# Taking the fourth head group's visit early, moving three half results to another buffer, and redrawing the scheduling settings in a fused attention and MLP kernel

## The chip, the cores and the metric

One core of one Trainium2 chip runs the whole program. The metric is the device time of one execution in microseconds. The engines are named as in the profile: PE (matmuls), PEld (the weight loads of PE), ACT (ScalarE), DVE (VectorE), POOL and SP (which issues the transfers). The kernel before took 1079.97 us, the median of 6 runs.

## The reference

It is a transformer block over 2048 tokens of width 1024: 32 query heads of width 32 that share one key and one value head, then an MLP with a sigmoid gate, each behind a layer norm and inside a residual sum.

```python
q = (ln(x) @ wq) -> 32 heads of 32;  k = ln(x) @ wk;  v = ln(x) @ wv      # one k, one v
p = softmax(q @ k.T * 32**-0.5);     h = x + (p @ v) @ wo
out = h + (sigmoid(ln(h) @ w_gate) * (ln(h) @ w_up)) @ w_down             # inner width 3584
```

## The kernel before

The program is built by a greedy planner that runs before compilation. It keeps an estimated clock for each engine and appends one instruction at a time to each engine's fixed list. Work on a query tile of 128 tokens is cut into **visits** (G, kq): head group G (8 heads of one query tile, so four groups make a tile) with key pair kq (256 keys). A visit is 8 score matmuls of 32 rows each and two exponentials of 128x1024. The first visits run while queries and keys are still being computed:

```python
visits = [(0, 0), (1, 0), (2, 0), (0, 1), (1, 1), (2, 1), (0, 2), (1, 2), (0, 3), (1, 3),
          (2, 2), (3, 0), (2, 3), (3, 1), (3, 2), (3, 3)]
visits += [(G, kq) for G in range(NX) for kq in range(VPH, VPG)]          # NX = 4: second halves
visits += [(G, kq) for G in range(NX, NT * ND) for kq in range(VPG)]
```

The first four groups are taken in two halves. The first half's result (values and row sums, 128x512 float32) is parked until the second half is there. Three lie in h_sb, the residual buffer, and the fourth in tnh:

```python
OcX = h_sb[...].bitcast(F32)                                 # three slots of 512 float32
def ocx(G, a, b):
    return OcX[:, G, a:b] if G < NH else tnh[:, a:b]         # NH = 3
```

Many instructions copy PSUM out, on ACT or on DVE, whichever is expected to be free first. One rule says how much queued work is counted:

```python
def evac(fn_act, fn_dve, n, deps, prio, dve_rate=0.96):
    now = pl.free["pe"]
    ready = now + 300.0 if v < 2 else 1e9                    # v: visits emitted so far
    a = max(pl.free["act"], now) + sum(o.occ for o in pl.heap["act"] if o.ready <= ready) + n / 1.2
    d = max(pl.free["dve"], now) + sum(o.occ for o in pl.heap["dve"] if o.ready <= ready) + n / dve_rate
    if a + (1000.0 * KNOBS[v // WIN][3] if v else 0.0) < d:  # ... ACT, else DVE
```

KNOBS holds 65 tuples of eight small integers, one tuple for each eight visits. They set thresholds and break ties in the planner. When nothing is ready for PE, the planner puts in **fillers**, matmuls whose result nobody reads:

```python
if 0 < v < 16 and not spare and known([exps[2 * v - 1]], t):
    ... mm(S_ps[:, k, 0:P], ident[:, :], ident[:, :], True, True), [c_id, exps[2 * v - 1]] ...
if v and spare:
    ... mm(F_ps[:, spare[0], 0:256], ident[:, :], kT4[:, 0:256], True, True) ...
```

The softmax here doesn't subtract the row's maximum and nothing guards it: scores larger than these inputs give would overflow.

## Time and profile before

| | before |
|---|---|
| median of 6 runs | 1079.97 us (1079.74 to 1080.29) |
| span of the profiled run | 1078.0 us |
| ACT busy, 60 to 1016 us | 955.18 of 956 us |
| last exponential ends | 1015.9 us |
| PE alone after that | 62 us |

A span is the time from the first to the last instruction, some 2 us less than the device time.

### The profile page before, as it was taken

To read this page: it belongs to the slowest core of one execution; us is meant where nothing else is said; L and a number is where in the kernel's file an instruction comes from. 1 tells how busy PE (TensorE), PEld (TensorE's weight loads), DVE (VectorE), ACT (ScalarE), POOL (GpSimd) and SP (SyncE) were. 2 spreads that over 40 slices of the span, in tenths; PEclk is the share of its full clock that TensorE was granted. 3 is DMA by queue.
4 is the path that set the end of the run, shared out by engine and by line. 5 is a ranking of instruction groups with operands and counts; after the bars stand their busy time and mean duration, and the time that the engine had idled before them with its cause. 6 is when DMAs were issued, how large, how long until landed. Compare 5 with 4: busy or idle time off the path is not lost.

```text
span 1078.0 us, 31453 instructions
## 1 busy us (share of the span) xinstructions
PE 1043.5 (97%) x12925; PEld 489.3 (45%) x13094; DVE 903.2 (84%) x1736; ACT 1009.8 (94%) x1167; POOL 30.6 (3%) x58
## 2 busy tenths in 40 slices
PE   8999999999999999999999999999999999999999
PEld 7764434444444444444444444444444444444445
DVE  7899999898989879898888989898887988888721
ACT  6999999999999999999999999999999999999700
POOL 2100000000000000000000000000000000000000
PEclk9999999999999999999999999999999999999999
DMA  7997898929679695959879594955969489896994
GB/s 222 183 293 249 209 290 237 280 70 286 164 210 240 153 262 125 267 141 253 198 187 261 138 267 113 285 161 157 265 164 276 109 232 199 208 234 161 294 277 106
DMA packets 308623, 227.14 MB, mean 211 GB/s; under 512 B 119808, under 2 KB 299904, under 8 KB 308480
## 3 DMA queue, kind: packets, MB, share of 16 engines
q1 hardware_dynamic: 307296, 224.92, 81.8%
q8 instruction: 103, 1.69, 0.7%
q14 instruction: 40, 0.33, 0.1%
q10 hardware_dynamic: 1184, 0.20, 0.1%
HBM read 195.17 MB, written 7.86 MB: 188 GB/s over the span
## 4 chain that ended last, share of the span: by engine, by line
PE 73%; ACT 19%; issue 4%; DVE 2%; DMA 1%; SPq 0%; DVEq 0%
PE F_ps L415 57%; ACT Pr L707 18%; PE S_ps L415 16%; ACT tnh L1009 1%; DVE Ts L741 1%; DMA ring<-in_B_w_up_dram 1%; DVE Rc L806 0%; DMA ring<-in_A_x_dram 0%; DVE st L346 0%; DVE Oc L796 0%; DVE hact L291 0%; DVE st L348 0%; PE F_ps L444 0%; DVE Oc L291 0%; DVE Ts L748 0%
## 5 line engine op out<-in xcount | busy, mean ns | idle before, releaser
L707 ACT ACTIVATE Pr<-S_ps 128x1024 bf16<-128x1024 f32 x1024 | 968.9, 1156 | 3.3 <-PE S_ps L415 2.6
L741 DVE TENSOR_TENSOR Ts<-Ts,Pr 128x1024 bf16<-128x1024 bf16 x736 | 481.5, 677 | 33.7 <-ACT Pr L707 31.4
L415 PE MATMUL F_ps<-ring,hnT 128*128 128x512 bf16 (+1 forms) x1870 | 400.7, 380 | 13.1 <-issue 8.5
L415 PEld LDWEIGHTS F_ps<-ring,hnT 128*128 128x128 bf16 (+1 forms) x1957 | 147.6, 97 | 189.5 <-issue 48.3
L415 PE MATMUL S_ps<-QTb,kT 32*128 32x256 bf16 x4096 | 206.2, 273 | 1.2
L415 PE MATMUL F_ps<-zone,hact 128*128 128x512 bf16 (+2 forms) x1106 | 197.5, 377 | 9.5 <-issue 9.0
L415 PEld LDWEIGHTS S_ps<-QTb,kT 32*128 32x128 bf16 x4096 | 63.1, 92 | 206.3 <-ACT Pr L707 153.4
L415 PE MATMUL F_ps<-Pr,Vb 128*32 128x256 bf16 x4064 | 134.2, 274 | 0.3 <-issue 0.3
L415 PEld LDWEIGHTS F_ps<-zone,hact 128*128 128x128 bf16 (+1 forms) x1164 | 75.0, 97 | 83.5 <-issue 23.0
L415 PEld LDWEIGHTS F_ps<-Pr,Vb 128*32 128x32 bf16 x4064 | 96.8, 96 | 29.9 <-issue 17.0
L741 DVE TENSOR_TENSOR Ts<-Pr 128x1024 bf16<-128x1024 bf16 x128 | 86.6, 684 | 25.6 <-ACT Pr L707 25.1
L1013 DVE SCALAR_TENSOR_TENSOR hst<-tnh,F_ps 128x512 bf16<-128x512 f32 x107 | 73.3, 685 | 38.3 <-PE F_ps L415 36.4
L1009 ACT ACTIVATE tnh<-F_ps 128x512 f32<-128x512 f32 x105 | 77.5, 738 | 5.7 <-PE F_ps L415 5.7
L415 PE MATMUL F_ps<-zone 128*128 128x256 bf16 (+4 forms) x658 | 72.2, 272 | 2.3 <-issue 1.1
L415 PE MATMUL F_ps<-wo_sb,OT 128*128 128x512 bf16 (+1 forms) x283 | 58.4, 380 | 1.7 <-issue 1.6
L415 PEld LDWEIGHTS F_ps<-zone 128*128 128x128 bf16 (+1 forms) x667 | 43.1, 97 | 22.8 <-issue 7.4
L748 DVE TENSOR_TENSOR Ts<-Ts 128x1024 bf16<-128x1024 bf16 x64 | 43.9, 686 | 1.1
L358 POOL TENSOR_SCALAR zb<-mvb 128x1 bf16<-128x1 bf16 (+1 forms) x25 | 9.9, 397 | 993.6 <-DVE mvb L350 993.6
L1009 ACT ACTIVATE tnh<-S_ps 128x512 f32<-128x512 f32 x7 | 4.2, 597 | 35.3 <-PE S_ps L415 35.3
L291 DVE COPY Oc<-F_ps 128x256 f32<-128x256 f32 x60 | 25.3, 422 | 11.6 <-PE F_ps L415 10.7
L415 PEld LDWEIGHTS F_ps<-wo_sb,OT 128*128 128x128 bf16 (+1 forms) x294 | 21.0, 97 | 26.2 <-issue 6.8
L796 DVE TENSOR_TENSOR Oc<-F_ps,Oc 128x256 f32<-128x256 f32 x59 | 24.9, 423 | 7.5 <-PE F_ps L415 6.4
(84 smaller groups left out, 415.4 us busy)
## 6 DMA issues: line engine op xcount, KB each, us to landing
ring<-in_B_w_gate_dram SPq DMA_DIRECT2D x318, 256.0 KB, 4.8
ring<-in_B_w_up_dram SPq DMA_DIRECT2D x316, 256.0 KB, 4.6
zone<-in_B_w_down_dram SPq DMA_DIRECT2D x28, 256.0 KB, 3.7
h_sb<-in_A_x_dram SPq DMA_DIRECT2D x16, 256.0 KB, 4.5
out_dram<-h_sb SPq DMA_DIRECT2D x31, 128.0 KB, 3.0
ring<-in_A_x_dram SPq DMA_DIRECT2D x7, 512.0 KB, 5.3
QTb<-q_scratch SPq DMA_DIRECT2D x14, 256.0 KB, 5.4
Pr<-in_B_w_gate_dram SPq DMA_DIRECT2D x10, 256.0 KB, 4.1
```

Of the source, the lines that this page charges most:

```text
L291: lambda: DVE.tensor_copy(out=out_ap, in_=in_ap))
L358: f = pl.op("pool", lambda: POOL.tensor_scalar(out=zb[:, ph, sl].unsqueeze(2), in0=mvb[:, ph, sl, 1:2], scalar1=LN_EPS_BF16, scalar2=None, ...
L415: fn = lambda: PE.matmul(o, lhsT=l, rhs=r, start=start, stop=stop, **kw)
L707: exps[u] = pl.op("act", lambda slot=slot, pb=pb: ACT.activation(out=pslot(slot).rearrange("p (a b) -> p a b", a=2), in_=S_ps[:, pb:pb + 2 ...
L741: o = pl.op("dve", lambda T=T, a=a, b=b: DVE.tensor_tensor(out=T, in0=a, in1=b, op=ALU.add), deps, prio=4, **t_dve(1024, 1.92))
L748: merge_ev[G] = pl.op("dve", lambda T4=T4: DVE.tensor_tensor(out=T4[:, :, 0, :], in0=T4[:, :, 0, :], in1=T4[:, :, 1, :], op=ALU.add), [sum ...
L796: a = pl.op("dve", lambda: DVE.tensor_tensor(out=Oc[:, :], in0=O, in1=Ob, op=ALU.add), [last, oc_ev[G], o_ev.get(G - 1)], prio=0, **t_dve( ...
L1009: tanh_of[n] = pl.op("act", lambda: ACT.activation(out=tnh[:, :], in_=FB(b), func=ACTF.Tanh, scale=0.5), [last, tn_user.get(0)] + (tn_more ...
L1013: e = pl.op("dve", lambda: DVE.scalar_tensor_tensor(out=hst[:, n % NST, :], in0=tnh[:, :], scalar=1.0, in1=FB(b), op0=ALU.add, op1=ALU.mul ...
```

## The change

The intent: keep ACT fed in the head by a visit that needs only keys already there, copy more of the early PSUM results on DVE, keep h_sb free of half results, and fit the tuples to the new course. The tuples are cut; the rest is whole.

```diff
-    KNOBS = [(4, 7, 0, 2, 2, 0, 0, 0), (0, 4, 0, 4, 1, 0, 0, 0), ...   # 65 tuples
+    KNOBS = [(4, 7, 1, 1, 3, 0, 0, 0), (3, 4, 1, 4, 3, 2, 0, 0), ...   # 65 other tuples
+        OcH = [hact[:, P + k * D:P + (k + 1) * D].bitcast(F32) for k in range(3)]
+        assert P + 3 * D <= NFT * P
         def ocx(G, a, b):
-            return OcX[:, G, a:b] if G < NH else tnh[:, a:b]
+            if G == 3:
+                return tnh[:, a:b]
+            return OcX[:, G - 3, a:b] if G > 3 else OcH[G][:, a:b]
-            ready = now + 300.0 if v < 2 else 1e9
+            ready = now + 300.0 if v < 4 else 1e9
-                    queues["Q" if t else "Q0"].append(mk_Q2(g, t))
+                    queues["Q0" if t == 0 or g < 2 * (NX - ND) else "Q"].append(mk_Q2(g, t))
-        visits = [(0, 0), (1, 0), (2, 0), (0, 1), (1, 1), (2, 1), (0, 2), (1, 2), (0, 3), (1, 3),
-                  (2, 2), (3, 0), (2, 3), (3, 1), (3, 2), (3, 3)]
+        visits = [(0, 0), (1, 0), (2, 0), (3, 0), (0, 1), (1, 1), (2, 1), (0, 2), (0, 3), (1, 2),
+                  (1, 3), (2, 2), (3, 1), (2, 3), (3, 2), (3, 3)]
+        visits += [(G, kq) for G in range(4, NX) for kq in range(VPH)]
         def xr_ready(t, deps):
-            if t < NH:
-                load_xr(t, deps)
-            else:
+            if t < 3:
+                oc_used.extend(deps)
+            elif t == 3:
                 tn_user[0] = deps[0]
                 tn_more.extend(deps[1:])
+            else:
+                load_xr(t - 3, deps)
+            if t == 2:
+                for k in [0] + list(range(NX - 3, NH)):
+                    load_xr(k, [])
+        oc_used = []
-                    [e] + ([d_last[t - 2]] if t > 1 else q_store[-NQS:] if t else []), prio=0, occ=800.0)
+                    [e] + ([d_last[t - 2]] if t > 1 else q_store[-NQS:] if t else oc_used), prio=0, occ=800.0)
```

More of the change, by code (lines that the diff above doesn't have):

```diff
@@ L170, in bass_sequential_preLN__grouped_kv_mqa__glu_gated_glu__prompt_kernel @@
     NCR = 12
-    KNOBS = [(4, 7, 0, 2, 2, 0, 0, 0), (0, 4, 0, 4, 1, 0, 0, 0), (2, 5, 0, 1, 3, 2, 1, 0), (3, 4, 1, 2, 3, 1, 1, 0), (3, 4, 0, 4, 2, 2, 1, 0), (1, 5, 1, 2, 3, 0, 1, 0), (4, 4, 0, 2, 2, 1, 0, 0), (4, 4, 1, 1, 3, 1, 1, 0), (1, 0, 0, 4, 3, 2, 0, 0), (3, 0, 1, 4, 2, 2, 0, 0), (1, 4, 1, 2, 3, 0, 1, 0), (4, 5, 0, 4, 2, 2, 0, 0), (3, 7, 0, 1, 3, 0, 0, 0), (2, 0, 1, 4, 2, 1, 0, 0), (3, 4, 0, 2, 2, 0, 1, 0), (2, 4, 0, 0, 3, 0, 1, 0), (3, 0, 0, 4, 3, 2, 0, 0), (2, 0, 0, 2, 3, 0, 1, 0), (0, 5, 0, 1, 3, 0, 0, 0), (1, 7, 1, 0, 3, 1, 0, 0), (0, 7, 0, 0, 3, 0, 1, 0), (2, 7, 0, 1, 3, 0, 0, 1), (4, 7, 0, 1, 3, 1, 1, 0), (1, 0, 1, 1, 3, 0, 0, 1), (4, 4, 0, 1, 3, 0, 0, 0), (3, 4, 1, 2, 3, 0, 1, 0), (2, 7, 0, 0, 3, 0, 1, 1), (0, 4, 1, 2, 2, 1, 1, 0), (3, 7, 1, 1, 2, 0, 1, 1), (4, 5, 0, 4, 3, 0, 0, 0), (4, 6, 0, 4, 3, 0, 0, 0), (2, 6, 1, 0, 3, 1, 1, 0), (1, 5, 1, 1, 2, 0, 1, 0), (4, 0, 0, 0, 2, 0, 0, 0), (4, 0, 0, 2, 3, 0, 1, 0), (2, 4, 0, 2, 2, 0, 1, 0), (0, 4, 0, 0, 3, 0, 0, 0), (3, 5, 0, 1, 2, 2, 0, 1), (1, 4, 0, 2, 2, 1, 1, 1), (4, 0, 0, 0, 3, 1, 0, 1), (1, 0, 0, 2, 3, 0, 0, 0), (2, 7, 0, 1, 3, 1, 0, 0), (3, 0, 0, 1, 2, 0, 0, 1), (1, 4, 0, 0, 3, 1, 1, 1), (0, 0, 1, 4, 2, 0, 0, 1), (3, 7, 0, 4, 3, 0, 0, 0), (1, 5, 1, 1, 2, 2, 0, 0), (4, 4, 0, 4, 2, 1, 1, 0), (0, 4, 0, 4, 3, 0, 1, 0), (1, 7, 0, 0, 2, 0, 1, 0), (1, 6, 0, 0, 3, 2, 1, 1), (2, 7, 0, 1, 3, 1, 0, 0), (4, 6, 1, 4, 2, 0, 0, 0), (0, 4, 0, 0, 2, 0, 0, 0), (4, 0, 0, 4, 3, 2, 1, 0), (3, 5, 1, 1, 3, 1, 0, 0), (2, 7, 0, 0, 3, 0, 0, 0), (3, 0, 0, 4, 2, 0, 1, 0), (4, 5, 0, 0, 3, 1, 0, 0), (4, 6, 0, 4, 1, 2, 0, 0), (4, 0, 0, 4, 3, 0, 0, 0), (4, 4, 0, 2, 2, 2, 0, 0), (4, 5, 0, 1, 1, 0, 1, 0), (4, 5, 1, 2, 2, 0, 0, 0), (2, 0, 0, 0, 2, 0, 0, 0)]
@@ new lines, in bass_sequential_preLN__grouped_kv_mqa__glu_gated_glu__prompt_kernel @@
+    KNOBS = [(4, 7, 1, 1, 3, 0, 0, 0), (3, 4, 1, 4, 3, 2, 0, 0), (2, 4, 0, 0, 2, 1, 1, 1), (2, 6, 0, 2, 2, 0, 0, 0), (2, 5, 1, 1, 2, 2, 0, 0), (3, 7, 1, 2, 3, 0, 1, 1), (1, 7, 0, 1, 2, 0, 1, 1), (3, 4, 1, 1, 3, 1, 1, 0), (1, 0, 1, 4, 2, 2, 0, 1), (3, 0, 0, 4, 3, 1, 0, 1), (3, 7, 0, 0, 3, 1, 1, 0), (4, 6, 1, 4, 3, 1, 1, 1), (1, 7, 0, 0, 3, 0, 1, 0), (2, 0, 0, 2, 3, 0, 1, 0), (3, 4, 0, 4, 3, 0, 1, 0), (2, 4, 0, 2, 3, 0, 0, 1), (2, 4, 0, 4, 3, 2, 1, 0), (2, 0, 1, 2, 3, 0, 1, 0), (1, 5, 0, 0, 3, 0, 0, 0), (3, 7, 1, 4, 3, 1, 1, 0), (3, 4, 1, 0, 2, 1, 1, 0), (2, 0, 1, 2, 2, 0, 0, 0), (1, 4, 0, 4, 2, 1, 1, 1), (4, 0, 1, 4, 3, 0, 0, 1), (2, 0, 0, 2, 3, 0, 0, 1), (0, 4, 1, 2, 3, 0, 0, 0), (2, 7, 0, 2, 3, 0, 1, 1), (4, 0, 1, 1, 2, 1, 1, 0), (0, 5, 0, 1, 3, 0, 1, 1), (3, 5, 0, 4, 1, 0, 0, 1), (3, 6, 0, 4, 3, 0, 0, 1), (2, 5, 1, 2, 3, 1, 1, 0), (1, 6, 1, 1, 3, 1, 1, 0), (4, 0, 0, 2, 2, 0, 0, 0), (4, 7, 0, 4, 3, 1, 0, 0), (2, 4, 1, 0, 2, 0, 0, 1), (4, 6, 0, 4, 2, 0, 0, 1), (1, 5, 0, 2, 3, 0, 0, 1), (0, 7, 0, 2, 2, 1, 1, 1), (3, 0, 0, 1, 3, 2, 1, 1), (0, 0, 0, 2, 2, 1, 0, 0), (2, 6, 0, 1, 3, 0, 0, 1), (4, 0, 0, 1, 3, 0, 0, 0), (0, 0, 0, 0, 3, 2, 1, 1), (1, 4, 1, 4, 2, 0, 1, 1), (3, 0, 0, 4, 3, 0, 1, 1), (4, 0, 0, 0, 3, 2, 1, 1), (4, 4, 0, 4, 2, 1, 1, 0), (3, 4, 0, 4, 3, 0, 1, 1), (4, 7, 0, 2, 3, 0, 1, 0), (3, 0, 0, 4, 3, 1, 1, 0), (2, 6, 1, 0, 2, 2, 0, 0), (2, 6, 0, 2, 2, 1, 1, 0), (4, 5, 0, 2, 3, 0, 0, 0), (2, 0, 0, 4, 2, 0, 0, 0), (4, 0, 1, 2, 3, 0, 0, 0), (0, 0, 0, 0, 3, 0, 1, 0), (2, 5, 0, 2, 2, 0, 1, 0), (2, 4, 0, 0, 2, 0, 0, 0), (4, 5, 0, 4, 3, 0, 1, 0), (4, 5, 1, 2, 2, 0, 0, 0), (4, 4, 0, 2, 3, 2, 0, 0), (4, 5, 0, 1, 1, 0, 1, 0), (4, 6, 1, 1, 2, 0, 1, 0), (2, 0, 0, 0, 1, 0, 1, 0)]
```

## The prediction

> **What bounds the kernel now.** I read the page's busy times, then its slices, then each engine in five stretches, and then the first 25 us instruction by instruction, because the change reorders only the beginning.
>
> The page's first part and two rows of its slices:
> ```profile
> span 1078.0 us, 31453 instructions
> ...
> PE 1043.5 (97%) x12925; PEld 489.3 (45%) x13094; DVE 903.2 (84%) x1736; ACT 1009.8 (94%) x1167; POOL 30.6 (3%) x58
> ...
> PE   8999999999999999999999999999999999999999
> ...
> ACT  6999999999999999999999999999999999999700
> ```
> Two engines look full, but they do not end together. ACT (the softmax exponentials) stops in the 38th slice; PE goes on alone to the end. The busy times by stretch, cut where I saw regimes change:
> ```profile
> 0.00:12.80 12.80, 10.53 (x157) 10.07 (x157) 8.85 (x25) 5.81 (x13) 3.42 (x14) 1.00 0.92 258
> 12.80:27.00 14.20, 12.14 (x208) 9.56 (x206) 12.61 (x35) 12.59 (x22) 2.29 (x5) 1.00 0.68 189
> 27.00:60.00 33.00, 32.97 (x579) 23.78 (x571) 26.20 (x72) 30.80 (x38) 4.18 (x8) 1.00 0.92 214
> 60.00:1016.00 956.00, 928.86 (x11618) 416.12 (x11781) 839.41 (x1578) 955.18 (x1088) 19.86 (x30) 1.00 0.83 211
> 1016.00:1078.00 62.00, 59.01 (x385) 29.75 (x383) 16.13 (x30) 5.37 (x9) 0.80 (x2) 1.00 0.77 203
> ```
> Columns are length, then PE, PEld, DVE, ACT and POOL busy, the clock and the DMA. From 60 to 1016 us ACT is busy 955.18 of 956: it sets when the exponentials end. PE fills the gaps between score matmuls with the gated MLP and is 97% busy in the same stretch. After 1016 there are no exponentials, and 62 us of projection and MLP matmuls are left. The end is therefore PE's total: its useful work plus what it wastes. An exponential issued earlier only moves the border between the fourth and fifth rows, unless PE loses less time.
>
> The chain that ended last says the same:
> ```profile
> PE 73%; ACT 19%; issue 4%; DVE 2%; DMA 1%; SPq 0%; DVEq 0%
> ```
> ACT holds 19% of it, in pieces among PE's. It is not a separate chain that could be shortened alone.
>
> Where does PE waste time? Of 34.5 us without a matmul (1078.0 − 1043.5), the waits of 60 to 1000 us put 20.0 us under "issue", 115 gaps of about 0.17 us; the change does not address these. The tail has 3.0 us, and 2.3 us lie before the first score. What an early reordering can reach lies between 14 and 24 us. PE there, in order of time:
> ```profile
> 14.49 0.40 PE L415 MATMUL S_ps<-QTb,kT 32*128 32x256 bf16 x8
> ...
> 16.46 0.89 PE L444 MATMUL F_ps<-ident,ring 128*128 128x128 bf16 x8 [0.69 <-ACT QTb L290]
> 17.87 0.68 PE L415 MATMUL S_ps<-ident 128*128 128x128 bf16 x9 [0.52 <-ACT Pr L707]
> ...
> 18.61 0.44 PE L415 MATMUL S_ps<-ident 128*128 128x128 bf16 x5
> ...
> 20.64 0.40 PE L415 MATMUL S_ps<-QTb,kT 32*128 32x256 bf16 x8
> ```
> The S_ps<-ident matmuls are dummies: identity by identity into a bank nobody reads, issued when no work is ready. They take 0.68 + 0.44 = 1.1 us; the bracketed waits are 0.69 + 0.52, and another of 0.76 us stands at 23.63. Sum: **3.1 us of PE waste**. From 27 to 60 us PE is busy 32.97 of 33, so nothing is to be had there. ACT in the same stretch:
> ```profile
> 17.65 1.75 ACT L290 ACTIVATE zone<-F_ps 128x512 bf16<-128x512 bf16 x3
> 19.98 0.38 ACT L290 ACTIVATE QTb<-F_ps 128x256 bf16<-128x256 f32 x1 [0.58 <-PE F_ps L415]
> 21.09 1.02 ACT L707 ACTIVATE Pr<-S_ps 128x1024 bf16<-128x1024 f32 x1 [0.72 <-PE S_ps L415]
> ```
> Between the fourth exponential (16.75) and the fifth (21.09) ACT evacuates PSUM for others and then idles 1.3 us. From 12.8 to 60 us ACT idles 1.61 + 2.20 = 3.8 us.
>
> **What the Trainium skill says.** "Perfetto Trace Analysis", section Identifying the Most-Contended Engine, says matmul busy share is a poor measure of headroom and points to weight-load busy. Here weight loads are 45% and matmuls 97%: the array is not at its peak, but no slot is free for another instruction stream. I use the busy share only to find gaps. "ScalarE: Activation LUTs", section What ACT_TABLE_LOAD costs, gives 186 ns + 0.833 ns per element for an ACTIVATE with immediate scale and bias, and about 93 ns of overlap back to back: for 1024 elements 1039 − 93 = 946 ns. The trace agrees: 968.9 us busy over 1024 is 946 ns. So exponentials have no slack, and ACT can only gain by starting earlier or doing less other work. "TensorEngine Tiling (Array Packing)", section Key Properties, says a change of tiling mode drains TensorE. The kernel changes mode around each 32-row score block and each 32-column output block; I cannot see the drain alone, but 8 score matmuls span 0.40 us. The same page, PSUM Bottleneck, advises evacuating with ScalarE and VectorE both; the 14-to-24 us rows show ACT doing most of it.
>
> **The change, part by part.**
>
> 1. Visit order. A visit is two score groups and two exponentials, about 1.9 us of ACT for 0.40 us of PE. The fourth visit was (0,1), needing the second key pair; now it is (3,0), needing the first. In the old trace the fourth score block starts at 22.48, just after the kT copy that it needs (22.01). The queries of head group 3 were copied at 16.00, so the new fourth visit can follow the third. This moves two exponentials up and delays the need for pairs 1 and 2 by one visit. Work added: none. The ninth visit still completes group 0, and at most 20 probability slots are filled before it, as before.
>
> 2. Half results in hact. Three of the first four groups' 128x512 float32 halves were copied to h_sb, the fourth to tnh; now three go to hact and the fourth still to tnh. The copies keep their size (0.68 to 0.69 us each, 2.1 us for the three in h_sb). The x rows for h_sb are loaded after group 2's second half instead of one by one. The old additions run at 65.3, 76.3, 85.3 and 90.2 us and the first residual addition at 99.72, so loads of 6.2 us issued near 86 still land first. The first hact transpose now also waits for those additions, tens of microseconds old by then (first MLP matmul: 112.76). **Value: 0.** It is capacity for more head groups, which NX = 4 does not use.
>
> 3. Two edits that select nothing: with NX = 4 and ND = 4 the test g < 2*(NX-ND) is g < 0, and range(4, NX) is empty. Value 0.
>
> 4. The evacuation chooser now counts only work ready within 0.3 us until the fourth visit, not the second. At visits 2 and 3 the old rule counted DVE statistics of rows not yet loaded and so favoured ACT. The 0.40 + 0.63 + 1.75 + 0.38 = 3.2 us of copies on ACT between 16.0 and 20.4 can partly go to DVE, which waited 1.55 us for x just before 16.45. The first window's ACT handicap falls from 2 to 1 us, which pulls the other way.
>
> 5. The 65 scheduling tuples are all new: in the head the fill threshold rises from 750 to 1000 ns and in the second window from 500 to 1000 ns, so scores are issued earlier. For the rest they redraw ties: which copies go to ACT, when an output block follows a score block, which MLP group goes first. They add no arithmetic, but they can change mode switches. About 1000 column-tiled pieces of 512 columns (432 + 364 + 72 + 60 + 36 + 32) are some 249 whole matmuls; in column form one costs 4 x 27.6/364 = 303 ns, in whole form 373.0/1506 = 248 ns. Ten per cent more or fewer is 25 x 55 ns = 1.4 us before any drain saved.
>
> Sum: of the 3.1 us PE waste I expect half, **−1.6 us**, since dummies vanish where the new score blocks (0.4 us each) and earlier evacuations fill them, while waiting for x remains. ACT may gain up to 3.8 us, but I count it 0: it turns into a longer PE tail. For the retuning I take **−0.8 us**, as settings fitted to this program should be no worse; that is a choice. 1079.95 − 2.4 = **1077.5 us**.
>
> **Rivals.** (a) ACT is the bound after all: all 3.8 us appear at the end, some 1076. For it: ACT 955.18 of 956. Against: 62 us of PE work follow the last exponential. (b) A new wait: two early exponentials sit before PSUM copies, or copies moved to DVE delay the normalization of later x rows; key pairs come late and PE idles in 20 to 40 us. For it: DVE is already 12.61 of 14.20 busy. It would give 1080 to 1082. (c) The retuning dominates: PE's 20 us of issue gaps, mode switches or weight-load waits (two, 1.3 us in all, on up-projection pieces between 100 and 220 us) shift by several microseconds either way, 1073 to 1083. (d) The head is hidden entirely: PE's work in 27 to 60 us absorbs all, 1079.5 to 1080.
>
> **Range and chances.** Head between 0 and −3.1, retuning between −4 and +2, both seldom extreme at once: 1073.5 to 1081. A 2% change is 21.6 us, seven times the PE waste in reach; so within 2% has 0.98, faster 0.015, slower 0.005.
>
> **What would show it.** Right: no or fewer S_ps<-ident dummies in 14 to 24 us; third and fourth score blocks near 17 to 20 us; more than 12 exponentials started before 30 us; the last exponential earlier by 1 to 4 us while PE's tail grows; PE's busy sum plus idle falls by 1 to 3 us. hact copies of 128x512 stay about 0.69 us, and no PE wait on h_sb loads near 95 us. Wrong: if the end moves as far as the last exponential (rival a), if PE waits on kT or x grow (b), or if the head is the same and the middle differs (c).

## More of the kernel before

"Busy" of PE is the union of its matmuls, whose ends are modelled, so short waits between matmuls can hide in it.

## The result, and the profile after

The kernel after takes **1078.71 us**, the median of 6 runs (1078.28 to 1080.75), against 1079.97. The ratio is 0.9991, 95% interval 0.9978 to 1.0004. Ratios here are the mean time of one kernel's runs over that of the other's in the same rounds, so not quite the ratio of the medians. The interval includes 1, so the gain of 1.3 us between medians is small against the scatter.

The page of the kernel after, first part and chain that ended last:
```profile
span 1076.4 us, 31527 instructions
...
PE 1066.6 (99%) x13035; PEld 489.1 (45%) x13035; DVE 903.2 (84%) x1734; ACT 1008.9 (94%) x1169; POOL 30.0 (3%) x58
...
PE 87%; ACT 7%; DVE 3%; issue 1%; DMA 1%; POOL 0%
```
Before you read 99% against 97% as an improvement, look at the counts. After has as many matmuls as weight loads, 13035. Before has 12925 against 13094: 169 matmul records are missing from that trace. Most of its "issue" gaps of about 0.17 us were matmuls without a record. A second trace of the same PE program, in the first experiment, shows it.

Busy times of the kernel after, in the stretches used for before (the last one ends at its span):
```profile
12.80:27.00 14.20, 12.78 (x215) 9.75 (x212) 13.31 (x37) 11.69 (x19) 2.50 (x5) 1.00 0.74 191
27.00:60.00 33.00, 32.42 (x573) 23.17 (x570) 25.80 (x69) 31.39 (x42) 3.91 (x8) 1.00 0.97 209
60.00:1016.00 956.00, 953.32 (x11746) 417.20 (x11745) 839.87 (x1578) 955.32 (x1090) 19.59 (x30) 1.00 0.82 212
1016.00:1076.40 60.40, 57.45 (x360) 28.75 (x358) 15.54 (x29) 4.78 (x8) 0.79 (x2) 1.00 0.80 204
```
ACT is as full as before from 60 to 1016 us, and what is shorter is the last row. From 12.8 to 60 us ACT idles 2.51 + 1.61 = 4.1 us, not less than the 3.8 us of before. PE's head, in order of time:
```profile
17.28 0.45 PE L420 MATMUL S_ps<-ident 128*128 128x128 bf16 x5 [0.30 <-ACT Pr L713]
...
17.80 0.44 PE L420 MATMUL S_ps<-ident 128*128 128x128 bf16 x5
...
19.83 0.40 PE L420 MATMUL S_ps<-QTb,kT 32*128 32x256 bf16 x8
...
22.55 0.45 PE L420 MATMUL S_ps<-ident 128*128 128x128 bf16 x5 [0.82 <-ACT Pr L713]
22.93 0.40 PE L420 MATMUL S_ps<-QTb,kT 32*128 32x256 bf16 x8
```
The third score block comes 0.8 us earlier (19.83 against 20.64), but the fourth, which no longer needs the second key pair, comes 0.45 us later (22.93 against 22.48). Counted from the first score block, which itself is 0.18 us later in this trace, that is 0.99 us earlier and 0.27 us later. The fourth stands behind a filler that waits for an exponential. ACT's copies shrank as intended, from 3.2 us between 16.0 and 20.4 us to 1.6:
```profile
17.09 0.63 ACT L295 ACTIVATE zone<-F_ps 128x512 bf16<-128x512 bf16 x1
18.00 0.60 ACT L295 ACTIVATE zone<-F_ps 128x512 bf16<-128x512 bf16 x1 [0.28 <-PE F_ps L449]
19.17 0.38 ACT L295 ACTIVATE QTb<-F_ps 128x256 bf16<-128x256 f32 x1 [0.58 <-PE F_ps L420]
```
Four exponentials now run in one piece before these copies. But the copies are in part only put off: from 27 to 60 us ACT makes 11 of them (42 instructions, 31 of them exponentials) where it made 7. So 12 exponentials have begun by 30 us and 40 by 60 us, before and after alike.

### The profile page after: what moved, and what is told of

The parts are those of the page before. It is cut to its first block, busy times and chain, and to the rows that moved or that the text cites. A ratio compares the mean times of both kernels' runs of the same rounds, so it can differ in the third digit from the quotient of the medians.

```text
span 1076.4 us, 31527 instructions
## 1 busy us (share of the span) xinstructions
PE 1066.6 (99%) x13035; PEld 489.1 (45%) x13035; DVE 903.2 (84%) x1734; ACT 1008.9 (94%) x1169; POOL 30.0 (3%) x58
## 4 chain that ended last, share of the span: by engine, by line
PE 87%; ACT 7%; DVE 3%; issue 1%; DMA 1%; POOL 0%
PE F_ps L420 69%; PE S_ps L420 18%; ACT Pr L713 7%; DVE Ts L747 1%; ACT tnh L1021 1%; DMA hact<-hst 0%; DMA ring<-in_A_x_dram 0%; DVE st L353 0%; DVE st L351 0%; DVE h_sb L905 0%; DVE ring L389 0%; DVE hact L790 0%; DVE hst L1025 0%; DVE ring L400 0%; DVE Rc L812 0%
## 5 line engine op out<-in xcount | busy, mean ns | idle before, releaser
L420 PE MATMUL F_ps<-ring,hnT 128*128 128x512 bf16 (+1 forms) x2011 | 417.3, 380 | 2.4 <-issue 1.8
L420 PE MATMUL F_ps<-zone,hact 128*128 128x512 bf16 (+1 forms) x1073 | 203.7, 380 | 0.1
L420 PEld LDWEIGHTS F_ps<-zone,hact 128*128 128x128 bf16 (+1 forms) x1073 | 71.7, 97 | 83.8 <-issue 21.1
L1021 ACT ACTIVATE tnh<-F_ps 128x512 f32<-128x512 f32 x104 | 80.3, 772 | 0.0
L420 PE MATMUL F_ps<-zone 128*128 128x256 bf16 (+5 forms) x655 | 74.5, 271 | 0.6 <-DVE hact L790 0.5
L420 PE MATMUL F_ps<-wo_sb,OT 128*128 128x512 bf16 (+1 forms) x315 | 61.7, 380 | 0.1
L818 DVE STREAM_TRANSPOSE Rc<-Ri 128x256 f32<-128x256 f32 x64 | 27.9, 437 | 0.1
```

The lines of the kernel that those rows point to most:

```text
L420: fn = lambda: PE.matmul(o, lhsT=l, rhs=r, start=start, stop=stop, **kw)
L818: d = pl.op("dve", lambda: DVE.transpose(out=Rc[:, :], in_=Ri[:, :].unsqueeze(2).to_broadcast([P, 2 * P // DH, DH])), [r], prio=pr, **t_dv ...
L1021: tanh_of[n] = pl.op("act", lambda: ACT.activation(out=tnh[:, :], in_=FB(b), func=ACTF.Tanh, scale=0.5), [last, tn_user.get(0)] + (tn_more ...
```

## The experiments

Two dates in each trace cut the time into three legs that add up: from the start to the first score block, from there to the last score block, and from there to the end. The first leg varies by some tenths with the arrival of the first x rows. The rows of these blocks on PE's timeline are in the profile of each run. Each row is one trace. Traces of the same PE program show how much a leg varies: the middle leg is 1000.00, 1000.39 and 1000.52 us in after, after_old_place and after_tail_split, and 1000.58 and 1000.12 us in before and place_only. So a difference of half a microsecond in this leg shows nothing by itself.

| run | to first score block | first to last | last to end | span |
|---|---|---|---|---|
| place_only (PE program of before) | 12.63 | 1000.12 | 64.6 | 1077.4 |
| tuples_only | 12.78 | 1001.27 | 64.0 | 1078.0 |
| after | 13.01 | 1000.00 | 63.4 | 1076.4 |
| after_old_place (PE program of after) | 12.71 | 1000.39 | 64.3 | 1077.4 |
| visits_only | 12.70 | 1001.12 | 76.1 | 1089.9 |
| after_old_visits | 12.77 | 999.26 | 69.7 | 1081.7 |
| after_old_evac | 12.83 | 1000.56 | 78.1 | 1091.5 |

### The placement alone

```diff
  kernel before, with the hunks for ocx, xr_ready, load_xr and oc_used, and the empty one for Q0, only
```

> The kernel before with only the half results moved into the activation buffer (visits, evacuation rule and tuples as before). Its TensorE and ScalarE programs are the same as before's, instruction for instruction. Theory (placement is worth 0): 1079.5 to 1080.5 us. Rival (the placement or the regrouped loads carry the gain): 1078.2 to 1079.2 us. Second question, records: if the 20.4 us of TensorE waits under 'issue' in the trace of before are lost matmul records (12925 matmuls against 13094 weight loads), this trace shows far fewer; if they are real gaps, it shows about 118 of them again.

Measured: 1079.82 us against 1079.79 us of before on the same chip, ratio 1.0001 (0.9989 to 1.0014). In the traces of the two, all 13094 weight loads and all 1167 ACT instructions come in the same order. The placement is worth nothing. Its profile holds the second answer:
```profile
PE 1067.5 (99%) x13094; PEld 489.6 (45%) x13094; DVE 903.0 (84%) x1736; ACT 1009.4 (94%) x1167; POOL 30.5 (3%) x58
...
PE F_ps L420 <- issue: 1.6, 6, 0.5
```
The same program with all its records shows 6 "issue" waits of 1.6 us in all, where the trace of before showed 118 of 20.4 us. The two edits that the prediction called empty were not run apart: with NX = ND = 4 the code asks for g < 0 in one and for an empty range in the other.

### The tuples alone

```diff
  kernel before, with only KNOBS of the kernel after
```

> The kernel before with only the 65 new scheduling tuples (visits, placement and evacuation rule as before). After about 60 us its TensorE program is the same as that of the kernel after. Theory (the gain comes from the tuples, the head gives nothing): 1078.4 to 1079.0 us, as the kernel after. Rival (the visit order in the head gives the gain): 1079.6 to 1080.3 us, as before.

Measured: 1080.42 us (1079.24 to 1080.76), ratio 1.0004 (0.9991 to 1.0016). **My theory fell here**: the tuples alone give nothing. PE's program after about 60 us is that of the kernel after, so the pair shows what visit order and evacuation rule are worth in the head under the new tuples. The first and the last score block of tuples_only and of after:
```profile
12.78 0.40 PE L415 MATMUL S_ps<-QTb,kT 32*128 32x256 bf16 x8
...
1014.05 0.40 PE L415 MATMUL S_ps<-QTb,kT 32*128 32x256 bf16 x8
```
```profile
13.01 0.40 PE L420 MATMUL S_ps<-QTb,kT 32*128 32x256 bf16 x8
...
1013.01 0.40 PE L420 MATMUL S_ps<-QTb,kT 32*128 32x256 bf16 x8
```
1001.27 against 1000.00 us. Of this, 1.06 us is there by the 65th exponential, near 82 us (each counted from the first score block), and the three traces of the PE program of after agree on it. From then on both engines run identical lists, so the lead is carried along; what comes on top is within the scatter of this leg.

The lead is less waiting, but not less than before. Waits of PE that have a line of their own, from the first score block to 62 us, add up to 1.97 us in place_only, 3.06 in tuples_only and 1.94 in after. Two of tuples_only stand in neither of the others:
```profile
36.37 0.29 PE L415 MATMUL S_ps<-ident 128*128 128x128 bf16 x2 [0.66 <-ACT Pr L707]
...
59.00 1.37 PE L415 MATMUL F_ps<-zone 128*128 128x256 bf16 x11 [0.43 <-ACT hact L290]
```
So under the new tuples the old order loses about a microsecond in the head, and the new order and rule make that good.

What the tuples do elsewhere shows when PE's span is split into streaming and the rest. In the tail of place_only a run of 28 matmuls of 512 columns takes 6.05 us to the next start, 216 ns each; in that of after 28 pieces of 32 array columns take 1.51 us, a quarter of that. Score matmuls of 32 rows are counted at a quarter as well, shorter ones by their columns. At these rates the matmuls whose results are read take 937.3 us in each of these traces. The remainder of the span, in us:

| run | fillers | rest: to first score block | next 70 us | to last score block | to end |
|---|---|---|---|---|---|
| place_only | 3.13 | 4.80 | 12.65 | 116.35 | 3.17 |
| tuples_only | 0.86 | 4.95 | 13.95 | 116.74 | 4.24 |
| after | 1.03 | 5.18 | 12.71 | 116.55 | 3.70 |
| after_old_place | 1.03 | 4.88 | 12.71 | 116.94 | 4.57 |

The kernel before has 22 fillers in the middle (2.4 us, one group near 404 us and one from 764 to 771); with the new tuples there are none, and the projections and the MLP have that time. This is the one clear saving against before, 2.1 us. The tail wait below, the first leg and the scatter take part or all of it back.

### The kernel after with the old placement

```diff
  kernel after, without the hunks for ocx, xr_ready, load_xr, oc_used and Q0
```

> The kernel after with the half results back in the residual buffer and the residual loads one by one; TensorE and ScalarE programs as in the kernel after. Theory (placement is worth 0): 1078.3 to 1079.2 us. Rival: the gain goes, 1079.6 to 1080.3 us. It also stands for a second sample of the kernel after beside tuples_only.

Measured: 1078.51 us (1078.05 to 1079.74), ratio 0.9990 (0.9978 to 1.0003). Again the placement does nothing. On the same chip it is 1.9 us below tuples_only.

### The kernel after without its fillers

```diff
+        lists["pe"] = [o for k, o in enumerate(lists["pe"]) if o.tag != "idle"]   # idle: the fillers
```

> The kernel after without the 19 filler matmuls (identity times identity) in the head, everything else in its order. In the trace of after one of them waits 0.82 us for an exponential at 22.55 us and the fourth score block stands behind it. Theory A (the filler itself holds the head back, and what the head gains reaches the end): the fourth score block comes about 1 us earlier and the time is 1077.3 to 1078.2 us. Theory B (the head gains, but the end is set by TensorE's total, so nothing arrives): score block earlier, time 1078.4 to 1079.0 us. Theory C (the next matmul waits for the same thing): nothing moves.

Measured: 1078.96 us (1077.78 to 1079.90), ratio 0.9994. In the trace the ninth to the 65th exponential start 0.3 to 0.5 us earlier than in after, measured from the first score block, so the fillers did hold the head back a little. The fourth score block comes 0.4 us earlier instead of 1 us: without the filler it waits itself, for 1.09 us. In the medians nothing arrives, though the scatter of 2 us would hide 0.5 us. This run does not decide between theories A and B.

### The tail

The last two runs had shown one more thing. After the last score block the schedule of after has less work left than that of before, but a new wait. PE in the tail of place_only, then of after; S_ps<-zone,hact and F_ps<-zone,hact are the two halves of a down projection, which reads transposed activations that arrive by DMA:
```profile
1022.84 3.62 PE L420 MATMUL S_ps<-ring,hnT 128*128 128x512 bf16 x16
1026.29 6.21 PE L420 MATMUL F_ps<-zone,hact 128*128 128x512 bf16 x28
```
```profile
1022.97 1.89 PE L420 MATMUL S_ps<-ring,hnT 128*128 128x512 bf16 x8
1024.70 5.34 PE L420 MATMUL S_ps<-zone,hact 128*128 128x512 bf16 x24
1030.53 1.04 PE L420 MATMUL S_ps<-zone,hact 128*128 128x512 bf16 x4 [0.49 <-DMA hact<-hst]
```
Before, 16 gate and up matmuls stood between the residual step and the down projection; after, 8 do. The last four matmuls of the first half then wait for the last transpose: 0.49 us here, 1.02 in tuples_only, 1.35 in after_old_place, 0 in after_no_dummies. I tried to take it away by putting other work before the four:

```diff
+        q = q[:e0 - 3] + q[e0 + 1:e1 - 3] + q[e0 - 3:e0 + 1] + q[e1 - 3:]   # e0, e1: the ends of the two halves
```

> The kernel after with one reordering in the tail: the last 4 of the 28 matmuls of the first half of tile 14's down projection are issued after the first 24 of the second half (other bank), so that they come 5 us later. Theory (after has a new wait there for the last transposed activations, 0.49 us in its trace, 1.35 and 1.02 us in those of after_old_place and tuples_only, absent in before): the wait is gone, 1077.4 to 1078.2 us, and the runs scatter less than the 1078.05 to 1080.75 us of after. Rival (the wait is hidden behind something else at the end): 1078.4 to 1079.0 us.

Measured: 1079.46 us (1077.97 to 1081.52), ratio 0.9996. The wait is gone and the time is not. Another came 30 us later:
```profile
1061.06 1.99 PE L420 MATMUL F_ps<-ring,hnT 128*128 128x512 bf16 x8 [0.66 <-DVE hst L1025]
```
DVE there waits for the hst buffers, which the transposes free, and these now take 5.6 us (median from issue to landing) against 4.2 us in after. The trace lists 19 weight loads of 256 KB issued after 1040 us beside them, against 15 in after, which may be the cause; no run tests it. The scatter grew instead of shrinking, from 2.5 to 3.6 us. After the last score block this trace needs 63.7 us against 63.4 in after: the reordering moved the wait, and no run shows what the tail would gain without any.

### One part at a time under the wrong tuples

```diff
  visits_only:      kernel before, with only the visit order of after
  after_old_visits: kernel after, with the visit order of before
  after_old_evac:   kernel after, with  ready = now + 300.0 if v < 2 else 1e9
```

> The kernel before with only the new visit order (tuples, evacuation rule and placement as before). Theory (parts add; the head order is worth about -1 us wherever it stands): 1078.3 to 1079.3 us. Rival (the tuples are indexed by visit and were fitted to one exact course; with another course they choose badly): slower than both kernels, 1082 to 1095 us, and the loss is spread over the middle, not in the head.

> The kernel after with the old visit order (new tuples, evacuation rule and placement). Theory (parts add): 1079.2 to 1080.2 us. Rival (fit to one course): 1082 to 1095 us.

> The kernel after with the old evacuation rule (all queued work counted from visit 2 on). Theory (parts add, the rule is worth a few tenths): 1078.5 to 1079.5 us. Rival (fit to one course): 1082 to 1095 us.

Measured: 1092.15 us (ratio 1.0113), 1084.14 us (1.0040) and 1093.64 us (1.0127), each within 0.8 us over its runs. The parts do not add. The reverted evacuation rule, a single constant, costs 15 us, more than ten times what the whole change brings. The last score blocks of visits_only and after_old_evac, each with its span:
```profile
span 1089.9 us, 31277 instructions
...
1013.82 0.40 PE L415 MATMUL S_ps<-QTb,kT 32*128 32x256 bf16 x8
```
```profile
span 1091.5 us, 31436 instructions
...
1013.39 0.40 PE L420 MATMUL S_ps<-QTb,kT 32*128 32x256 bf16 x8
```
These are within 1.1 us of place_only's 1012.75. The exponentials finish on time, and nearly the whole loss is work that PE had not done by then: 76 and 78 us are left instead of 64.6. This is the best evidence for what sets the end.

Why did PE do less in the same time? I took the distance from each matmul's start to the next and subtracted its columns at the streaming rate, as above. Against place_only, visits_only loses 12.2 us more this way, nearly the whole difference of 12.5. (after_old_evac loses 11.6 us more and has 2.5 us more fillers.) Of it 6.9 us lie between whole-array matmuls, 4.4 of them in waits above 0.15 us and the rest in shorter gaps, and some 1.1 us net at changes of tiling mode. One cause can be counted: an output block directly after a score block needs one mode change less than one after MLP work. In the traces, 14 output blocks stand behind MLP work in before, 9 in after, 26 in after_old_visits, 30 in after_old_evac and 41 in visits_only. The remaining 4 us lie inside the score and output blocks; where they and the 6.9 us come from I leave open.

### The kernel before without its fillers

```diff
  kernel before, with the line shown for the kernel after without fillers
```

> The kernel before without its 36 identity fillers (14 in the head, 22 in the middle of 0.11 us each), everything else in its order. Theory A (the fillers stand in real waits; the next matmul waits for the same thing): 1079.3 to 1080.2 us. Theory B (they hold TensorE back, so dropping them is what the kernel after gains in the middle): 2.4 us in the middle and up to 1.1 in the head less, 1076.8 to 1078.2 us.

Measured: 1081.60 us (1079.92 to 1082.50), ratio 1.0015 (1.0001 to 1.0029): slower, which neither theory had. The granted clock explains it. PE busy is the first number after the length, the clock the third from the end; place_only, then before_no_fillers:
```profile
16.00:20.00 4.00, 3.13 (x46) 2.75 (x47) 3.49 (x8) 3.41 (x7) 0.15 (x1) 1.00 0.77 273
20.00:24.00 4.00, 3.24 (x64) 2.40 (x63) 4.00 (x13) 3.27 (x7) 0.79 (x2) 1.00 0.14 25
```
```profile
16.00:20.00 4.00, 2.23 (x22) 1.68 (x23) 3.53 (x8) 3.54 (x7) 0.20 (x1) 0.84 0.77 270
20.00:24.00 4.00, 4.00 (x57) 3.10 (x54) 4.00 (x13) 1.67 (x4) 0.74 (x2) 0.73 0.16 27
```
Without fillers the mean clock falls to 0.84 and 0.73 in these stretches; in windows of 1 us it is 0.50 from 19 to 22 us, and the 23 matmuls that took 1.82 us in place_only take 3.33 us there. The program is 1.5 us late by the ninth exponential, counted from the first score block. The Trainium skill, "TensorE: Matmul & The Clock Gate", Part 1, says the throttle is the default state and activity lifts it; the trace agrees, for the 0.50 follows the 3 us in which PE was busy 0.39 to 0.44 of the time. The run of 1079.92 us is the only one of the five with a mean clock of 1.000; it equals before. In the middle, dropping 22 fillers changes nothing: the lag behind place_only, counted the same way, is 1.46 us at the 257th exponential and 1.56 us at the last. So they stand in real waits, and leaving them out gains nothing; the kernel after has none there because its tuples put other work in that time.

No run beats the kernel after clear of noise.

## Why the prediction was right or wrong

The time, 1078.71 us, lies in the range, and "same" was given 0.98. Both were easy to meet: the range of 1073.5 to 1081 contains the kernel before, too. The gain was put at 2.4 us and is 1.3 us between medians, and the 95% interval of the ratio includes no gain at all. Neither of its two terms came about as told, so that the sum has the right sign is partly luck.

**What bounds the kernel: right.** The prediction held that the end is PE's total, and that the last exponential only marks a border. visits_only and after_old_evac show it: the border moves by about 1 us, the end by 12 and 14 us. Rival (a), ACT as the bound, falls.

**The head, −1.6 us: failed against before.** The step was that new score blocks and earlier copies would take half of PE's 3.1 us of fillers and waits. Instead the head fillers went from 14 to 19, the named waits from 1.97 to 1.94 us, and in the first 70 us after the first score block PE gets 0.3 us less useful work done than in place_only. Of the signs named beforehand, a fourth score block near 17 to 20 us (22.93), more than 12 exponentials by 30 us and a longer PE tail did not appear. The 33rd exponential does start 1.02 us earlier than in place_only, but the 513th 1.17 us later, and the last 0.12 us earlier, which is nothing. A head lead of 1.06 us is real only against tuples_only, where it makes good what the tuples lose; from there it is 1.7 to 1.9 us between medians, in ranges that overlap and with the tail wait in them. The early copies did move, three of six from ACT to DVE. Which of visit order and rule brought the 1.06 us stays open, since either alone spoils the rest of the schedule.

**The retuning, −0.8 us: failed as a term of its own.** "Settings fitted to this program should be no worse" was argued for the whole program, and then added as if the tuples had a value of their own. Alone they cost 0.6 us between medians of the same chip, a difference within the noise. They remove the 22 fillers in the middle, which the prediction didn't look at, and leave 1.7 us less work behind the last score block (62.9 against 64.6 us in the traces, waits taken off). But they bring the new tail wait of 0 to 1.4 us and, with the old visit order, 1.3 us of waits and gaps in the head. The tuples belong to one exact course of the planner. The 55 ns that the prediction put on the column form is too much: its busy times hold modelled ends. From the start of one run of such matmuls to what follows, four pieces take 264 ns in place_only and a whole matmul 231 (from 60 us on).

**Fillers as waste: wrong in the head of before.** There 1.1 of the 3.1 us were fillers, and without them the clock falls and the end comes later. In the head of after they cost 0.3 to 0.5 us in the traces.

**The 20 us under "issue": misread.** I took 115 gaps for time that the change does not address. They were lost records, and the missing count stood in the page: 12925 matmuls, 13094 weight loads. It did no harm to the sum.

**Placement 0, dead edits 0: right**, the first by two runs, the second by the code; the edit for Q0 was also in place_only, whose order on PE and ACT is that of before. The rival of a new wait (b) came true in small: in the head 0.82 us for an exponential at 22.55 us and twice 0.26 us for a copy on DVE (at 41.60 and 48.97), not for key pairs, and in the tail up to 1.35 us.

## What to carry to other kernels

When two engines are both full, find the one that has work left after the other's last instruction; shifting the other one's work moves only the border between them. In a list-scheduled kernel whose settings are fitted to one course, an edit tried alone measures mostly the misfit (5 to 15 us here), so judge it with the settings refitted, or where both programs become identical again. Before you delete work that nobody reads, check the granted clock without it.

## What the Trainium skill lacked or had wrong

- "TensorE: Matmul & The Clock Gate": its rule of thumb is to have no idle gaps of PE above about 3.4 us. Here the clock fell to half with shorter ones: in the run without fillers PE was busy 0.39 to 0.44 of each microsecond from 16 to 19 us, its longest wait was 1.01 us, the clock was 0.50 from 19 to 22 us, and the kernel lost 1.8 us. A later part of the page does tell of a kernel whose clock fell after many short idle times, but gives no busy share. Whether a busy share over some 3 us is the better rule, this one event cannot show.
- "TensorEngine Tiling (Array Packing)", Key Properties: it says that a mode change drains TensorE, without a size. Here, in after, six MLP matmuls start at 1011.62 us and stream for 6 x 0.216 = 1.30 us; the score block starts at 1013.01, 0.09 us later, and the next whole-array matmul 0.33 us after the block's start.
- "Perfetto Trace Analysis": it warns of matmul busy time, but not of missing matmul records. 169 of 13094 looked like nearly 19 us of waits (20.4 us under "issue" against 1.6), and comparing the counts of matmuls and weight loads shows it at once.
